# VectorE's port operations wait for GpSimd's turn, as GpSimd's already wait for VectorE's

## The chip, the cores and the metric

The kernel runs on one core of one Trainium2 chip. A core has five engines that run side by side, each through its own list of instructions in order: TensorE (PE in the profile, its weight loads apart as PEld), VectorE (DVE), ScalarE (ACT), GpSimd (POOL) and SyncE (SP, which only issues DMAs here). They wait for each other by semaphores. The metric is the device time of one execution in microseconds; the time before is the median of three runs.

## The reference

Attention over 8 batches of 8 heads (576 rows, head size 64), in which every score further than `tau` below its row's largest is left out, and behind it a gated mix: a causal convolution of 5 taps over the attention's output makes a gate, and two 512x512 products make the output.

```python
# attention: q, k, v are (8, 8, 576, 64)
scores = scale * q @ k.T
thresh = max(scores, axis=-1) - tau
scores = where(scores >= thresh, scores, -1e9) - max(scores)
attn = exp(scores) / (sum(exp(scores)) + 1e-9)
x = (attn @ v)            # heads joined: (8, 576, 512)
# mix
gate = sigmoid(sum(conv_w[k] * xp[:, k:k + 576] for k in range(5)))
out = (gate * (x @ w_val)) @ w_out
```

## The kernel before, in words

Two heads make a pair; a batch has four pairs. For a pair, TensorE makes tiles of 128 rows of scores (line 641) in PSUM, where four buffers called `u` serve everything that TensorE writes. VectorE scales each tile into `sb` and takes its largest value in the same instruction (`largest`, line 651). ScalarE makes the exponential `e` (670 and 672). What lies under the threshold is then left out in one of two ways: on VectorE (`keep`, line 689: reads `sb` and `e`, writes `pp` or `pl`) or on ScalarE (`bend`, 683). TensorE transposes the result (782), ScalarE or VectorE copies it to SBUF as `T` (794), TensorE multiplies it with `v` (855, or 826 in the first pairs), and VectorE brings the product to SBUF as `xT` (864 or 832).

The mix splits each float32 operand into a high and a low part, for products in three passes: `xh`, `xl` of `xT` (361 or 898, and 904 on GpSimd), `gh`, `gl` of the gated value (1074, and 1082 on GpSimd). The first tap of the convolution is on GpSimd (917), further ones on VectorE (`tap`, 922: reads `xT` and `pre`, writes `pre`); some of the first batches' are on GpSimd (937, 943). The products of a batch (line 1013) run on TensorE among the score tiles of the next batch. In the first 150 us the weights too are put together from 64-bit words, on VectorE (374 to 387), ScalarE and GpSimd (385, 390, 436). GpSimd also makes some thresholds `th` (663) and widens reciprocals (`inv`, 722).

The order of all this is made by a planner. Each operation is recorded with its engine, a cost and a due time, and `carry_out` plays them out on a model of the engines in which VectorE's operations on SBUF alone (engine name "DVEp": lines 374 to 387, 689 and 922) and all of GpSimd's ("POOL") take turns at one shared `port`. The instructions are then written out in that planned order. Beyond the waits that the data need, `carry_out` adds one kind of wait by hand: each operation on GpSimd also waits for the DVEp operation that the plan put last before it. VectorE's operations that read PSUM (651, 794, 864, 1051, 1115) have no part in the turns.

Of the kernel before, what the change touches and what calls it, by code (L numbers as in the profile page):

```python
# [35 lines left out]
for x in range(6):  # L36
# [10 lines left out]
    s=3,  # L47
# [19 lines left out]
    turn=-4538.24, copy=-712.99, attend=-3389.02, evac=-2135.73, fetch=1749.39, high_k=-1420.92,  # L67
# [13 lines left out]
def tile_thresholded_attention_gated_mix(  # L81
# [104 lines left out]
    port = [0.0]  # L186
# [16 lines left out]
    def keep_busy(room, n, x=ident):  # L203

        for _ in range(n):
            nc.tensor.matmul(room[:, 0:P], x, x, start=True, stop=True, skip_group_check=True)

    def sent(t, n, latency, each):

        at = t  # L210
        for _ in range(n):
            if len(landings) >= 8:
                at = max(at, landings[-8])
            wire[0] = max(wire[0], at + latency) + each
            landings.append(wire[0])
            at += SEND
        return at - t, wire[0] - t

    def carry_out():
        done_ops = []  # L220
        while True:
            best = None
            for e, ops in open_ops.items():
                can = []
                free = idle[e.rstrip("p")]
                if e in ("DVEp", "POOL"):
                    free = max(free, port[0])
                for o in ops:
                    if all(r.times for r in o.takes):
                        can.append((max([free, o.ready] + [r.times[0] for r in o.takes]), o))  # L230
                if can:
                    t = min(x for x, _ in can)
                    o = min((x[1] for x in can if x[0] <= t), key=(lambda o: o.due + AVOID * CHANGE.get((shape[0], o.shape), 0.0)) if e == "PE" else lambda o: o.due)
                    if best is None or (t, o.due) < (best[0], best[1].due):
                        best = (t, o, e)
            if best is None:
                break
            t, o, e = best
            for x in o.ways:
                open_ops[x].remove(o)  # L240
            if e == "PE" and 0.0 < idle["PE"] and t < FILL_UNTIL:
                pause = t - idle["PE"]
                if pause > 0.5:
                    o.fill = int((pause - 0.25) / 0.24)
            cost, done, emit = o.ways[e]
            if e == "PE" and cost:
                extra = CHANGE.get((shape[0], o.shape), 0.0)
                cost, done = cost + extra, done + extra
                shape[0] = o.shape
            if isinstance(done, tuple):  # L250
                cost, done = sent(t, *done)
            o.port = e if e in ("DVEp", "POOL") else None
            if o.port:
                port[0] = t + cost
            e = e.rstrip("p")
            idle[e] = t + cost
            o.landed, o.engine = t + done, e
            done_ops.append((o, emit))
            for r in o.takes:
                r.times.pop(0)  # L260
            for r, _ in o.gives:
                r.times.append(o.landed)
                r.times.sort()
            for n in o.next:
                n.ready = max(n.ready, idle["PE"] if e == "PE" and e in n.ways else o.landed)
                n.waits -= 1
                if not n.waits:
                    for x in n.ways:
                        open_ops[x].append(n)
        assert not any(open_ops.values()), "some operations can never begin"  # L270
        emitting.append(True)
        shared = None
        for o, emit in done_ops:
            if o.fill and r_right.live:
                keep_busy(r_right.live[-1][:, 1, PAST :], o.fill)
            n = len(nc.cur_bb.bb.instructions)
            emit()
            made = [x for x in nc.cur_bb.bb.instructions[n:]] if o.port else ()
            if made and o.port == "POOL" and shared:
                tc.add_manual_dep(  # L280
                    made[0], shared.name, mybir.DependencyInfo(mybir.DependencyClass.Sync, mybir.DependencyReason.DATA),
                    reason="VectorE's turn at the shared port is over",
                )
            elif made and o.port == "DVEp":
                shared = made[0]
            for rooms, room in o.gives:
                rooms.give(room(), o.landed)

# [245 lines left out]
    class Tile:  # L534
        s = None
# [65 lines left out]
        def room(self):  # L601

            if self.s is None:
                self.s = self.grp.second
            return self.s
# [555 lines left out]
    at = 0  # L1161
# [6 lines left out]
    for t in jobs:  # L1168
# [21 lines left out]
        if t.pair.g == NP - 1:  # L1190
            last = products(batch, len(tiles), last)
    carry_out()


# [57 lines left out]
```

## Time and profile before

| what | value |
|---|---|
| median of 3 runs | 684.32 us (684.11 to 684.62) |
| the profiled execution's own time | 684.27 us |
| its span, first to last instruction | 682.5 us |
| TensorE busy | 663.4 us, 97% of the span |
| VectorE busy | 604.1 us, 89% |
| ScalarE busy | 556.9 us, 82% |
| GpSimd busy | 223.1 us, 33% |
| TensorE's granted clock | 0.999 of full speed |

The 1.8 us between the profiled execution's time and its span lie outside the instructions. A busy engine is not always one that sets the time: a busy share is an average over stages. Which engine is waited for is read from the chain of waits and from the timeline.

### The profile page before, as it was taken

The numbers are of one execution on the slowest core, as the hardware profiler recorded it, in microseconds if no ns is written. First come the engines' busy times: TensorE is split into PE (matmuls) and PEld (weight loads), VectorE is DVE, ScalarE is ACT, GpSimd is POOL, SyncE is SP. The second block draws the span as 40 slices with busy tenths as digits, with TensorE's granted clock in tenths as the row PEclk, the third lists the DMA queues.
The fourth block names the chain that finished last, engine by engine and source line by source line (L and its number), as shares of the span: only waits on it lengthen the run. The fifth ranks groups of instructions, "written<-read, shape, count | busy, mean of one in ns | idle before, by whom it ended". The sixth has DMA issues, their size and how long they took to land.

```text
span 682.5 us, 21511 instructions
## 1 busy us (share of the span) xinstructions
PE 663.4 (97%) x8668; PEld 527.7 (77%) x8668; DVE 604.1 (89%) x1592; ACT 556.9 (82%) x1152; POOL 223.1 (33%) x383
## 2 busy tenths in 40 slices
PE   9999899989999999999999999999999999999997
PEld 6566566786887778888787788877788887877897
DVE  6999999977999999999999998998999999999742
ACT  6999999996878898787878888888987878788420
POOL 1454543565132421233222322324213332223131
PEclk9999999999999999999999999999999999999999
DMA  7133332321322223223321223221232233210002
GB/s 271 52 117 100 117 119 86 118 69 54 123 88 88 72 71 122 69 87 105 122 83 43 87 103 122 88 88 48 95 112 79 87 105 120 65 63 2 37 36 70
DMA packets 21075, 61.18 MB, mean 90 GB/s; under 512 B 2928, under 2 KB 4336, under 8 KB 20976
## 3 DMA queue, kind: packets, MB, share of 16 engines
q1 hardware_dynamic: 20832, 59.62, 25.8%
q8 instruction: 68, 1.11, 0.7%
q14 instruction: 31, 0.25, 0.1%
q10 hardware_dynamic: 144, 0.20, 0.1%
HBM read 50.37 MB, written 9.44 MB: 88 GB/s over the span
## 4 chain that ended last, share of the span: by engine, by line
PE 70%; DVE 15%; ACT 9%; issue 2%; DMA 0%; POOL 0%; DVEq 0%; ACTq 0%
PE u L1013 29%; PE u L641 18%; PE u L855 15%; PE u L782 8%; DVE sb L651 4%; DVE pre L922 3%; ACT T L794 3%; DVE pp L689 2%; ACT e L672 2%; ACT e L670 1%; ACT pp L683 1%; DVE T L794 1%; DVE g L1051 1%; DVE xT L864 1%; DVE sums L708 0%
## 5 line engine op out<-in xcount | busy, mean ns | idle before, releaser
L651 DVE TENSOR_SCALAR_CACHE_REDUCE sb<-u,sc 128x576 f32<-128x576 f32 x288 | 229.0, 810 | 14.8 <-PE u L641 10.7
L641 PE MATMUL u<-k,q 64*128 64x288 f32 x1240 | 192.9, 421 | 6.6 <-DVE sb L651 2.2
L670 ACT ACTIVATE e<-sb,th 128x576 f32<-128x576 f32 x165 | 124.7, 770 | 29.2 <-DVE th L663 21.0
L855 PE MATMUL u<-T,v 128*64 128x256 f32 (+1 forms) x1080 | 136.7, 408 | 0.7 <-DVE sb L651 0.7
L641 PEld LDWEIGHTS u<-k,q 64*128 64x128 f32 x1240 | 108.7, 188 | 27.3 <-DVE sb L651 7.3
L683 ACT ACTIVATE pp<-e,minus 128x576 f32<-128x576 f32 x142 | 109.6, 772 | 22.9 <-DVE pp L689 22.3
L782 PEld LDWEIGHTS u<-ident,pp 64*128 64x128 f32 x2304 | 99.0, 139 | 29.9 <-ACT pp L683 5.1
L855 PEld LDWEIGHTS u<-T,v 128*64 128x64 f32 x1080 | 75.2, 137 | 59.6 <-ACT T L794 6.5
L794 ACT COPY T<-u 128x768 f32<-128x768 f32 (+1 forms) x162 | 110.4, 699 | 11.0 <-PE u L782 9.8
L782 PE MATMUL u<-ident,pp 64*128 64x64 f32 x2304 | 109.4, 225 | 3.5 <-ACT T L794 0.9
L922 DVE SCALAR_TENSOR_TENSOR pre<-xT,cw,pre 128x576 f32<-128x576 f32 x121 | 100.5, 832 | 2.4 <-POOL pre L943 1.4
L689 DVE SCALAR_TENSOR_TENSOR pp<-sb,th,e 128x577 f32<-128x577 f32 x114 | 97.2, 856 | 3.8 <-ACT e L672 3.0
L672 ACT ACTIVATE e<-sb,nm 128x576 f32<-128x576 f32 x123 | 93.9, 771 | 0.2
L1013 PE MATMUL u<-gh,woh 64*128 64x288 f32 x512 | 88.9, 332 | 0.6 <-ACT seen L1001 0.3
L1013 PE MATMUL u<-xh,wvh 64*128 64x288 f32 x512 | 88.2, 326 | 0.5 <-ACT seen L1001 0.4
L794 DVE COPY T<-u 128x512 f32<-128x512 f32 (+1 forms) x94 | 73.9, 792 | 9.7 <-ACT e L670 5.0
L1082 POOL TENSOR_TENSOR gl<-g,gh 128x288 fp32r<-128x288 f32 x64 | 51.0, 803 | 89.8 <-DVE sums L708 34.4
L1013 PE MATMUL u<-xh,wvl 64*128 64x288 f32 x512 | 79.8, 292 | 0.0
L1013 PE MATMUL u<-xl,wvh 64*128 64x288 f32 x512 | 79.6, 292 | 0.0
L1013 PE MATMUL u<-gh,wol 64*128 64x288 f32 x512 | 78.8, 292 | 0.0
L1013 PE MATMUL u<-gl,woh 64*128 64x288 f32 x512 | 78.7, 292 | 0.0
L722 POOL TENSOR_SCALAR inv<-r 128x128 f32<-128x128 f32 x64 | 20.0, 312 | 159.8 <-DVE r L712 65.6
(95 smaller groups left out, 1037.8 us busy)
## 6 DMA issues: line engine op xcount, KB each, us to landing
q<-qT SPq DMA_DIRECT2D x31, 608.0 KB, 3.9
k<-kT SPq DMA_DIRECT2D x31, 496.0 KB, 4.8
v<-vs SPq DMA_DIRECT2D x32, 320.0 KB, 2.9
outT<-o SPq DMA_DIRECT2D x28, 288.0 KB, 2.1
pre<-w_val SPq DMA_DIRECT2D x4, 512.0 KB, 5.9
pre<-w_out SPq DMA_DIRECT2D x4, 512.0 KB, 3.3
outT<-o SPq DMA_DIRECT2D x8, 144.0 KB, 1.8
pp<-first SPq DMA_DIRECT2D x2, 192.0 KB, 3.0
```

The lines of the kernel that those rows point to most:

```text
L641: nc.tensor.matmul(row(self.s)[:, a, :], t.q[rows, x : x + P], t.k[rows, k0 : k0 + HS], start=i == 0, stop=h is not None or i == 1, skip_g ...
L651: nc.vector.tensor_scalar(self.sb[:, :S].rearrange("p (a f) -> p a f", a=2), row(self.room()), sc, None, op0=ALU.mult, op1=ALU.min, accum_ ...
L670: nc.scalar.activation(y, x, AF.Prelu, bias=self.grp.th[:, i : i + 1], scale=-1.0, alpha=STEEP)
L672: nc.scalar.activation(y, x, AF.Exp, bias=self.grp.nm[:, i : i + 1], scale=-1.0)
L683: nc.scalar.activation(grp.p[:, i * S : (i + 1) * S], self.e[:, :S], AF.Exp, bias=minus, accum_out=grp.sums[:, i : i + 1])
L689: nc.vector.scalar_tensor_tensor(grp.p[:, i * S : (i + 1) * S + 1], self.sb, grp.th[:, i : i + 1], self.e, op0=ALU.is_le, op1=ALU.mult, ac ...
L782: nc.tensor.transpose(tp[:, r, i * APART_BY : i * APART_BY + D], x[rows, :], ident[rows, rows])
L794: engine(T[:, c0 : c0 + n, self.off : self.off + P].rearrange("p c (r q) -> p r c q", r=2), tp)
L855: nc.tensor.matmul(a[hs, : W[half.j]], t.v[:, c0 : c0 + D], half.T[:, 2 * NKC if c == NKC else h * NKC + c, 0 : W[half.j]], start=c == 0, ...
L922: engine.scalar_tensor_tensor(cv, pair.xT[:, i + a : i + z], cw[:, g, i : i + 1], cv, op0=ALU.mult, op1=ALU.add)
L1013: nc.tensor.matmul(made["room"][:, to, 0:HS], wt[rows, c, e * P : (e + 1) * P], moving(c, i)[rows, parts[j]], start=turn == c == n == 0, s ...
L1082: engine.tensor_sub(gs[e][1][:, c], g[x][:, c], gs[e][0][:, c].bitcast(F32))
```

## The change

Before, only GpSimd's operations had the added wait. Now the same rule holds for both sides: `carry_out` remembers the last operation at the port, of whichever engine, and when the engine changes, the new one's first instruction waits for that operation. For GpSimd this is the wait that it had (a second operation in a row needs none, since it follows its own engine's first). New are the waits of VectorE's port operations for the GpSimd operation that the plan puts ahead of them. No instruction is added, removed or moved to another place on its engine.

```diff
             made = [x for x in nc.cur_bb.bb.instructions[n:]] if o.port else ()
-            if made and o.port == "POOL" and shared:
-                tc.add_manual_dep(
-                    made[0], shared.name, mybir.DependencyInfo(mybir.DependencyClass.Sync, mybir.DependencyReason.DATA),
-                    reason="VectorE's turn at the shared port is over",
-                )
-            elif made and o.port == "DVEp":
-                shared = made[0]
+            if made:
+                if shared and shared[0] != o.port:
+                    tc.add_manual_dep(
+                        made[0], shared[1].name,
+                        mybir.DependencyInfo(mybir.DependencyClass.Sync, mybir.DependencyReason.DATA),
+                        reason="the other engine's turn at the shared port is over",
+                    )
+                shared = (o.port, made[0])
```

In the built program, 99 rows of VectorE's list held a wait for GpSimd before, and 146 do now. In 140 places a VectorE instruction now has to see the end of a later GpSimd operation than it had to before; in some of these the row reads alike, because it waited for an earlier GpSimd operation already. All 140 are at lines 374 to 387, 689 and 922.

The first place is on VectorE in the fifth batch: the taps of one pair (`pre0<-xT0`, line 922) among the score tiles of the next. Before (in brackets, the engines that a row waits for; Activation is ScalarE, Pool is GpSimd):

```order
L922 SCALAR_TENSOR_TENSOR pre0_151<-xT0_138,cw0_176,pre0_151 128x576 [waits DVE_49]
L708 TENSOR_SCALAR sums2_124<-sums2_124 128x1 [waits Activation_49]
L651 TENSOR_SCALAR sb1_107,nm2_112<-u1_95,sc_78 128x576 [waits PE_49]
L712 RECIPROCAL r2_129<-sums2_124 128x2 [waits DVE_49]
L922 SCALAR_TENSOR_TENSOR pre0_151<-xT0_138,cw0_176,pre0_151 128x576
L689 SCALAR_TENSOR_TENSOR pp1_119,sums1_123<-sb0_106,th0_114,e1_105 128x577 [waits Activation_49]
```

Now (every line number below the change is one higher):

```order
L923 SCALAR_TENSOR_TENSOR pre0_151<-xT0_138,cw0_176,pre0_151 128x576 [waits DVE_49]
L709 TENSOR_SCALAR sums2_124<-sums2_124 128x1 [waits Activation_49]
L652 TENSOR_SCALAR sb1_107,nm2_112<-u1_95,sc_78 128x576 [waits PE_49]
L713 RECIPROCAL r2_129<-sums2_124 128x2 [waits DVE_49]
L923 SCALAR_TENSOR_TENSOR pre0_151<-xT0_138,cw0_176,pre0_151 128x576 [waits Pool_49]
L690 SCALAR_TENSOR_TENSOR pp1_119,sums1_123<-sb0_106,th0_114,e1_105 128x577 [waits Activation_49]
```

The second tap here, which waited for nothing, now waits for GpSimd (for `gl1<-g1,gh1`, line 1082); the rows stand where they stood.

The second place is a little earlier on VectorE, behind another pair's attention. Before:

```order
L922 SCALAR_TENSOR_TENSOR pre1_152<-xT1_139,cw0_176,pre1_152 128x576
L712 RECIPROCAL r2_129<-sums2_124 128x2 [waits DVE_49]
L689 SCALAR_TENSOR_TENSOR pp1_119,sums1_123<-sb3_109,th2_116,e0_104 128x577 [waits Activation_49,Pool_49]
L922 SCALAR_TENSOR_TENSOR pre1_152<-xT1_139,cw0_176,pre1_152 128x576 [waits DVE_49]
L708 TENSOR_SCALAR sums1_123<-sums1_123 128x1 [waits Activation_49]
L712 RECIPROCAL r0_127<-sums1_123 128x2 [waits DVE_49]
L922 SCALAR_TENSOR_TENSOR pre1_152<-xT1_139,cw0_176,pre1_152 128x576
```

Now:

```order
L923 SCALAR_TENSOR_TENSOR pre1_152<-xT1_139,cw0_176,pre1_152 128x576 [waits Pool_49]
L713 RECIPROCAL r2_129<-sums2_124 128x2 [waits DVE_49]
L690 SCALAR_TENSOR_TENSOR pp1_119,sums1_123<-sb3_109,th2_116,e0_104 128x577 [waits Activation_49]
L923 SCALAR_TENSOR_TENSOR pre1_152<-xT1_139,cw0_176,pre1_152 128x576 [waits DVE_49]
L709 TENSOR_SCALAR sums1_123<-sums1_123 128x1 [waits Activation_49]
L713 RECIPROCAL r0_127<-sums1_123 128x2 [waits DVE_49]
L923 SCALAR_TENSOR_TENSOR pre1_152<-xT1_139,cw0_176,pre1_152 128x576 [waits Pool_49]
```

Two taps have got a wait for GpSimd (for `xl`, line 904, and for `gl`, line 1082), and the `keep` between them has lost its own, because the first tap now waits for the same engine later than it did.

## Rows read from the trace of the kernel before

**Rows 1.** Head of the page: span of the profiled execution.

```profile
span 682.5 us, 21511 instructions
```

**Rows 2.** Windows: from:to, length, then busy us of PE, PEld, DVE, ACT, POOL.

```profile
20.00:40.00 20.00, 19.67 (x222) 13.11 (x221) 18.85 (x55) 19.94 (x41) 10.19 (x16) 1.00 0.32 101
367.40:447.40 80.00, 79.45 (x1076) 64.62 (x1074) 74.35 (x194) 66.86 (x141) 23.07 (x43) 1.00 0.27 90
```

**Rows 3.** Line 922: count, shortest/median/longest ns, first and last start.

```profile
L922 DVE SCALAR_TENSOR_TENSOR pre<-xT,cw,pre x121: 793/814/1299, 33.8 to 655.0; 128x576 f32<-128x576 f32 x121
```

**Rows 4.** Timeline near 170 us: start, length, engine, line, [idle before <-releaser].

```profile
168.85 1.43 POOL L943 TENSOR_TENSOR pre<-pre,tmp 128x576 f32<-128x576 f32 x1
...
170.26 0.76 POOL L917 TENSOR_SCALAR pre<-xT,cw 128x576 f32<-128x576 f32 x1
...
170.31 1.30 DVE L922 SCALAR_TENSOR_TENSOR pre<-xT,cw,pre 128x576 f32<-128x576 f32 x1 [0.26 <-POOL pre L943]
```

**Rows 5.** Timeline: first and last of the 61 late places, VectorE's instruction.

```profile
11.44 0.18 DVE L380 TENSOR_SCALAR cw<-cw 128x20 int32<-128x20 int32 x1
...
653.35 0.81 DVE L922 SCALAR_TENSOR_TENSOR pre<-xT,cw,pre 128x576 f32<-128x576 f32 x1
```

**Rows 6.** Chain that ended last, 442 to 453 us: start, length, what.

```profile
442.52 0.75 DVE g L1051
...
450.42 0.60 DVE T L794
```

**Rows 7.** Timeline of the same place: GpSimd, VectorE, TensorE.

```profile
447.10 0.80 POOL L1082 TENSOR_TENSOR gl<-g,gh 128x288 fp32r<-128x288 f32 x1 [4.89 <-DVE sums L708]
...
447.75 0.80 DVE L922 SCALAR_TENSOR_TENSOR pre<-xT,cw,pre 128x576 f32<-128x576 f32 x1
...
451.07 0.76 PE L641 MATMUL u<-k,q 64*128 64x288 f32 x4 [0.22 <-DVE sums L708]
```

**Rows 8.** Timeline, 386 to 392 us: GpSimd, VectorE, TensorE.

```profile
386.04 0.73 POOL L904 TENSOR_TENSOR xl<-xT,xh 128x256 fp32r<-128x256 f32 x1
...
386.43 0.95 DVE L922 SCALAR_TENSOR_TENSOR pre<-xT,cw,pre 128x576 f32<-128x576 f32 x1
...
388.10 0.81 DVE L922 SCALAR_TENSOR_TENSOR pre<-xT,cw,pre 128x576 f32<-128x576 f32 x1
...
389.06 0.79 POOL L1082 TENSOR_TENSOR gl<-g,gh 128x288 fp32r<-128x288 f32 x1 [2.29 <-DVE pre L922]
...
389.50 0.97 DVE L922 SCALAR_TENSOR_TENSOR pre<-xT,cw,pre 128x576 f32<-128x576 f32 x1
...
390.79 0.94 DVE L794 COPY T<-u 128x768 f32<-128x768 f32 x1
...
392.03 0.51 PE L1013 MATMUL u<-gh,woh 64*128 64x288 f32 x2
392.37 0.30 PE L1013 MATMUL u<-gl,woh 64*128 64x288 f32 x2
```

**Rows 9.** Timeline, 151 to 159 us: GpSimd, VectorE, TensorE.

```profile
151.83 0.86 POOL L904 TENSOR_TENSOR xl<-xT,xh 128x320 fp32r<-128x320 f32 x1
...
152.05 3.44 DVE L922 SCALAR_TENSOR_TENSOR pre<-xT,cw,pre 128x576 f32<-128x576 f32 x4
...
155.58 1.42 POOL L943 TENSOR_TENSOR pre<-pre,tmp 128x576 f32<-128x576 f32 x1 [2.88 <-DVE sums L708]
156.96 0.25 POOL L361 TENSOR_SCALAR pl<-pl 128x64 f32<-128x64 f32 x1
...
157.03 0.82 DVE L922 SCALAR_TENSOR_TENSOR pre<-xT,cw,pre 128x576 f32<-128x576 f32 x1 [0.53 <-POOL pre L943]
...
158.64 1.57 PE L855 MATMUL u<-T,v 128*64 128x320 f32 x10 [0.73 <-DVE sb L651]
```

**Rows 10.** Timeline: first and last of five GpSimd operations behind a running VectorE one.

```profile
15.40 0.76 POOL L663 TENSOR_SCALAR th<-nm,less 128x1 f32<-128x1 f32 x1 [1.82 <-DVE r L712]
...
166.78 1.43 POOL L904 TENSOR_TENSOR xl<-xT,xh 128x320 fp32r<-128x320 f32 x1 [1.00 <-DVE pre L922]
```

## The prediction

> **What bounds the kernel now.** I read the windows first. In a period of 80 us, one of the batches in the middle that repeat, TensorE is busy 79.45 us and VectorE 74.35 us [rows 2]. So the middle is TensorE's, with 0.55 us to spare, and VectorE has 5.65 us. In the first 140 us it is otherwise: ScalarE is busy 19.94 of 20 us, TensorE 19.67 and VectorE 18.85 [rows 2]; there ScalarE sets the pace. Next I read the chain of waits, since a bound by busy time still passes through other engines. Once in each period it leaves TensorE: for 8.5 us, from 442.52 to 451.02, it runs over VectorE alone, without a gap, and gives back to TensorE behind a copy [rows 6]. What makes VectorE late there makes the end late. Last I read the timeline, for where a VectorE operation begins before the GpSimd operation has ended that it will now wait for.
>
> **What the change removes and adds.** It moves nothing. It adds 140 waits of VectorE, of which I paired each with the two instructions in the timeline. In 79 places GpSimd's operation had ended over 0.03 us before VectorE's began: these cost nothing as long as the two stay that far apart. In 61 it had not; the first and the last are in [rows 5], and 30 of them lie in the first 200 us.
>
> **The price of a late place.** A wait for GpSimd is short: VectorE starts at 170.31, 0.03 us behind GpSimd's end at 168.85 + 1.43 = 170.28 [rows 4]. A tap usually takes 0.814 us [rows 3]. So with the wait VectorE's end is 0.03 + 0.81 = 0.84 us behind GpSimd's. What is it without? The same instruction at 170.31 runs into GpSimd's next one, 170.26 to 171.02, takes 1.30 us and ends at 171.61, 0.59 us behind it [rows 4]. The two are kept apart already, but the blocked VectorE operation has its beginning behind it when the port comes free: the wait costs 0.84 - 0.59 = 0.25 us that the port doesn't. Where the overlap is under about 0.2 us nothing was lengthened, and the wait costs the overlap and 0.03 us more. For each of the 61 I took the later of its own start and GpSimd's end + 0.03, added its usual length, and subtracted its old end: 13.2 us in all, 7.5 of them in the first 200 us and 5.8 behind. That is VectorE's lateness if nothing takes it up, the upper bound of this term; the lower one is 0.
>
> [...]
>
> **What of it is on the path.** Behind a waiting instruction stands all of VectorE's list: the next tiles' `largest` (line 651), which frees a `u` for TensorE, the copies to `T` (794) and to `xT` (864).
>
> (a) In each period the tap at 447.75 lies in the stretch where the chain is VectorE's. GpSimd's `gl` ends at 447.10 + 0.80 = 447.90; the tap may start at 447.93 and ends at 448.74, not at 448.55 [rows 7]. Nothing takes the 0.19 us up: the next three instructions and the copy follow each other without a gap, and the copy ends at 451.02 [rows 6], and TensorE, idle for 0.22 us, starts 0.05 us behind that, at 451.07 [rows 7]. Six such places, 208 to 608 us: 1.1 us.
>
> (b) In each period there is a pair of late taps, at 386.43 and 389.50. The first may start at 386.04 + 0.73 + 0.03 = 386.80 and ends at 387.61, not at 387.38; the tap at 388.10 follows 0.23 us late and ends at 389.14. GpSimd's `gl` waits for that one already: it begins 0.15 us behind its end [rows 8], now at 389.29, and ends at 390.08. So the tap at 389.50 starts at 390.11 and ends at 390.92, not at 390.47: 0.45 us late, for the wait goes to and fro. The copy at 390.79 ends at 392.18, not at 391.73. TensorE's products start at 392.03 [rows 8], 0.30 us behind the old end; in (a) 0.05 were enough. So they may be 0.20 us late. But their first row takes 0.51 us and the next one 0.30 [rows 8], so the first may have stood 0.21 us in the queue for the array anyway. Between 0 and 0.20 us I take 0.10, the row deciding for neither; six places: 0 to 1.2, taken as 0.6 us.
>
> (c) At 152.05 four taps begin under GpSimd's `xl`, which ends at 152.69: by the price above, about 0.23 us more here, all four end that much later. GpSimd's addition at 155.58 follows the taps and ends at 157.00 + 0.23; GpSimd's `pl`, 0.25 us long, follows that one, and the tap at 157.03, which waited only for the addition, now waits for `pl` too: until about 157.47. That is 0.44 us; the `largest` behind it frees what TensorE has been waiting for 0.73 us, at 158.64 [rows 9]. 0.4 us, once.
>
> (d) The other 28 places of the first 200 us hold about 6.9 us. VectorE has 1.15 us idle in 20 us there, and ScalarE has none [rows 2], so most of it lies beside ScalarE's work; bounds 0 and 6.9. I take 0.6, near the lower end for that reason.
>
> (e) The other places of a period, some 0.3 us, lie in VectorE's 5.65 us of idle time [rows 2]. If that cover went, each would cost up to 0.25 us.
>
> Sum: 1.1 + 0.6 + 0.4 + 0.6 = 2.7 us. The profiled execution took 684.27 us, with a span of 682.5 us [rows 1], and lies 0.05 us under the median, 684.32. Forecast: **687.0 us**, 0.4% slower; with (a) and (c) alone 685.8, with (b) at 1.2 and (d) at 4 of its 6.9 us, 691.
>
> **The rivals.** This kernel's runs tell a change from none at about 0.2%, 1.4 us.
>
> *Lateness is taken up (no change), 684.3 to 685.7.* For it: VectorE is not the bound by busy time, and 0.55 us of TensorE's idle time in a period [rows 2] hide 0.19 us if TensorE isn't short of buffers. Against: (a) and (c) sit where TensorE is seen waiting. [...] Chance of both 0.17.
>
> *Waits go to and fro: over 691.* Since GpSimd waits for VectorE and VectorE for GpSimd, a late operation on either makes the other late, as in (b) and (c), and places that are early now become late. With all 13.2 us on the path 697.5 us. Against: in the middle VectorE's idle time, 5.65 us a period, is over five times the lateness there (5.8 us in some six periods). Chance 0.08.
>
> *Faster.* In five places of the first 170 us GpSimd began while VectorE held the port, out of the plan's turn, and was held up itself: a threshold at 15.40 took 0.76 us, an `xl` at 166.78 took 1.43 us [rows 10] where the same shape takes 0.86 [rows 9]; these are the first and the last of the five. Against the usual lengths of their kinds they lose 2.5 us together; now GpSimd goes first. If these thresholds and reciprocals are what ScalarE and TensorE wait for in the stretch that ScalarE bounds, and none of (a) to (d) comes through: 681.8 us. It decides from 1.4 us net. Against: (a) alone takes back 1.1. Chance 0.07.
>
> That the change does nothing is excluded: the waits stand in the built program.
>
> **The numbers.** Forecast 0.68 (685.7 to 691), taken up 0.17, to and fro 0.08, faster 0.07. So slower by over 0.2% 0.76, within 0.2% 0.17, faster 0.07. The range leaves out the two outer cases and the lowest part of the second: 684.6 to 691 us.
>
> **What would show it.** Right: no tap or `keep` is longer than 0.85 us; in the stretch of (a) VectorE idles for GpSimd once a period, about 0.2 us; in (c) TensorE's 0.73 us become about 1.15; a period takes 80.2 to 80.4 us; GpSimd's five operations have their usual lengths. Wrong: the period stays at 80.0 while VectorE's idle time for GpSimd grows, which says that (a) is taken up; or the loss lies in the first 140 us, which says that (d) was put too low.

## The result, and the profile after

The changed kernel takes 689.36 us (median of 4 runs, 689.29 to 689.45), beside 684.47 us (684.11 to 684.88) for the kernel before on the same chip: a ratio of 1.0074 [1.0062, 1.0086]. It is slower by 4.9 us, 0.7%. The forecast was 687.0 us in a range of 684.6 to 691.0, so the direction and the range held, and the forecast itself lay 2.4 us low.

The head of the page after, to compare with [rows 1]:

```profile
span 687.5 us, 21491 instructions
```

Two windows after, beside [rows 2]; the second one is the same period, 4.3 us later at its start and 4.5 at its end (from:to, length, then busy us of PE, PEld, DVE, ACT, POOL):

```profile
20.00:40.00 20.00, 19.47 (x220) 12.85 (x217) 18.26 (x56) 19.60 (x40) 10.18 (x16) 1.00 0.30 101
371.70:451.90 80.20, 79.43 (x1076) 64.31 (x1074) 73.88 (x194) 66.97 (x142) 23.08 (x43) 1.00 0.26 90
```

In the first window all three busy engines have lost time: TensorE 0.20 us, VectorE 0.59, ScalarE 0.34. ScalarE, which had 0.06 us idle in 20, now has 0.40. In the period VectorE is busy 0.47 us less, because the time for which a tap or a `keep` was held up under GpSimd's operation counted as busy and a wait doesn't (in the period the lines of the tap and the `keep` are busy 13.30 and 11.19 us before, 13.03 and 10.68 after): a lower busy share is no gain here.

The taps after, beside [rows 3] (shortest, median and longest ns), and one of the reasons for which VectorE sat idle before them (us, times; these six are the second taps of (b)):

```profile
L923 DVE SCALAR_TENSOR_TENSOR pre<-xT,cw,pre x121: 806/816/822, 34.3 to 660.2; 128x576 f32<-128x576 f32 x121
...
  POOL gl L1083: 2.1, 6
```

The longest tap takes 0.822 us, not 1.299. No tap is blocked any more, and the time stands as idle time in front of it.

The place (a) on the timeline after, beside [rows 7]: GpSimd, VectorE, TensorE (start, length, engine, line, [idle before <-releaser]):

```profile
451.34 0.80 POOL L1083 TENSOR_TENSOR gl<-g,gh 128x288 fp32r<-128x288 f32 x1 [4.88 <-DVE sums L709]
...
452.18 0.82 DVE L923 SCALAR_TENSOR_TENSOR pre<-xT,cw,pre 128x576 f32<-128x576 f32 x1
...
455.52 0.76 PE L642 MATMUL u<-k,q 64*128 64x288 f32 x4 [0.44 <-DVE sums L709]
```

GpSimd ends at 452.14 and the tap starts at 452.18. From GpSimd's start to the tap's it was 0.65 us, now 0.84: 0.19 us, as worked out. TensorE's idle time grows from 0.22 to 0.44 us. This is the place as predicted.

The pair of (b) after, beside [rows 8]:

```profile
390.24 0.73 POOL L905 TENSOR_TENSOR xl<-xT,xh 128x256 fp32r<-128x256 f32 x1
391.01 0.82 DVE L923 SCALAR_TENSOR_TENSOR pre<-xT,cw,pre 128x576 f32<-128x576 f32 x1
...
393.50 0.79 POOL L1083 TENSOR_TENSOR gl<-g,gh 128x288 fp32r<-128x288 f32 x1 [2.53 <-DVE pre L923]
...
394.33 0.82 DVE L923 SCALAR_TENSOR_TENSOR pre<-xT,cw,pre 128x576 f32<-128x576 f32 x1 [0.36 <-POOL gl L1083]
...
396.47 0.40 PE L1014 MATMUL u<-gh,woh 64*128 64x288 f32 x2
396.71 0.30 PE L1014 MATMUL u<-gl,woh 64*128 64x288 f32 x2
```

The wait does go to and fro: tap, GpSimd's `gl`, tap, each behind the other. But TensorE's first row of products takes 0.40 us where it took 0.51, and the second one starts at 396.71, 4.34 us later than before, when the score tile ahead of it was already 4.29 us late: the pair costs 0.05 us.

The place (c) after, beside [rows 9]:

```profile
154.88 0.87 POOL L905 TENSOR_TENSOR xl<-xT,xh 128x320 fp32r<-128x320 f32 x1
155.78 3.00 DVE L923 SCALAR_TENSOR_TENSOR pre<-xT,cw,pre 128x576 f32<-128x576 f32 x4 [0.60 <-POOL xl L905]
...
160.25 0.24 POOL L362 TENSOR_SCALAR pl<-pl 128x64 f32<-128x64 f32 x1
160.53 0.82 DVE L923 SCALAR_TENSOR_TENSOR pre<-xT,cw,pre 128x576 f32<-128x576 f32 x1 [0.74 <-POOL pl L362]
...
162.14 2.91 PE L856 MATMUL u<-T,v 128*64 128x320 f32 x20 [1.09 <-DVE sb L652]
```

The tap starts behind GpSimd's `pl`, and TensorE idles 1.09 us instead of 0.73.

And GpSimd's two operations of [rows 10]:

```profile
15.37 0.27 POOL L664 TENSOR_SCALAR th<-nm,less 128x1 f32<-128x1 f32 x1 [1.99 <-DVE r L713]
...
170.25 0.87 POOL L905 TENSOR_TENSOR xl<-xT,xh 128x320 fp32r<-128x320 f32 x1 [1.00 <-DVE pre L923]
```

They take 0.27 and 0.87 us instead of 0.76 and 1.43: GpSimd now goes first, as worked out.

**Where the 4.9 us are.** I follow four rows of TensorE through every profile: A, score products at the start (line 625, `u<-pp,pl`, 8.12 us before, in the profile of the kernel before), B, a transposition that waits for VectorE's reciprocal (line 782, 151.48), C and D, the ends of (c) and of (a) in [rows 9] and [rows 7] (158.64 and 451.07). In the kernel before it takes 143.36 us from A to B, 7.16 from B to C and 292.43 from C to D. A and B before, and after:

```profile
8.12 1.19 PE L625 MATMUL u<-pp,pl 64*64 64x288 f32 x8
...
151.48 0.53 PE L782 MATMUL u<-ident,pp 64*128 64x64 f32 x10 [0.33 <-DVE r L712]
```

```profile
7.61 1.19 PE L626 MATMUL u<-pp,pl 64*64 64x288 f32 x8
...
154.53 0.53 PE L783 MATMUL u<-ident,pp 64*128 64x64 f32 x10 [0.45 <-DVE r L713]
```

After, A starts at 7.61, so A to B takes 146.92 us: 3.56 more. B to C takes 0.45 more and C to D 0.95 more. The table says the same of every kernel below; times are medians, beside 684.4 to 684.5 us for the kernel before. The ratio goes by all runs of both kernels and so need not be the quotient of the medians.

| kernel | time, us | ratio to before | A | A to B | B to C | C to D |
|---|---|---|---|---|---|---|
| after | 689.36 | 1.0074 [1.0062, 1.0086] | 7.61 | +3.56 | +0.45 | +0.95 |
| early | 688.18 | 1.0051 [1.0034, 1.0067] | 8.27 | +3.41 | +0.46 | +0.22 |
| late | 685.99 | 1.0023 [1.0012, 1.0035] | 7.92 | +0.03 | +0.01 | +0.91 |
| passed | 685.37 | 1.0009 [1.0000, 1.0019] | 7.42 | +1.29 | +0.02 | +0.48 |
| not_passed | 688.65 | 1.0057 [1.0040, 1.0073] | 8.12 | +2.40 | +0.46 | +0.96 |
| slow_vector | 684.81 | 1.0006 [0.9997, 1.0015] | 8.40 | +0.44 | 0.00 | +0.05 |
| slow_vector2 | 687.25 | 1.0051 [1.0039, 1.0064] | 8.55 | +2.66 | +0.01 | -0.05 |
| slow_scalar | 690.32 | 1.0086 [1.0072, 1.0099] | 8.51 | +5.19 | -0.01 | +0.29 |
| nowaits | 690.52 | 1.0090 [1.0076, 1.0104] | 7.76 | -0.79 | +0.63 | +3.64 |
| one_way | 686.75 | 1.0040 [1.0027, 1.0053] | 7.71 | +0.58 | +0.84 | +1.08 |
| late_turns | 683.44 | 0.9990 [0.9981, 0.9999] | 7.77 | -0.83 | +0.01 | +0.08 |
| cut_once | 689.43 | 1.0070 [1.0056, 1.0084] | 8.62 | +2.90 | +0.44 | +0.91 |

A itself moves by up to 1.2 us from one profile to the next, whatever the kernel (last section), so single times are compared behind A. How well two profiles agree from there on is seen in late, whose program up to 190 us is that of before: from A to B it stays within 0.06 us of it, at points 20 us apart.

### The profile page after: what moved, and what is told of

Its sections match the earlier page's. It is cut to its first block, busy times and chain, and to the rows that moved or that the text cites. A ratio compares the mean times of both kernels' runs of the same rounds, so it can differ in the third digit from the quotient of the medians.

```text
span 687.5 us, 21491 instructions
## 1 busy us (share of the span) xinstructions
PE 663.3 (96%) x8668; PEld 526.3 (77%) x8668; DVE 599.8 (87%) x1592; ACT 558.6 (81%) x1152; POOL 220.6 (32%) x383
## 4 chain that ended last, share of the span: by engine, by line
PE 71%; DVE 13%; ACT 7%; POOL 3%; issue 2%; DMA 0%; DVEq 0%; POOLq 0%
PE u L1014 29%; PE u L642 18%; PE u L856 15%; PE u L783 8%; DVE pre L923 4%; DVE sb L652 3%; DVE pp L690 3%; ACT T L795 2%; ACT e L671 2%; ACT pp L684 1%; ACT e L673 1%; PE u L827 1%; DVE T L795 1%; POOL gl L1083 1%; DVE xT L865 1%
## 5 line engine op out<-in xcount | busy, mean ns | idle before, releaser
L923 DVE SCALAR_TENSOR_TENSOR pre<-xT,cw,pre 128x576 f32<-128x576 f32 x121 | 98.4, 815 | 9.3 <-POOL pre L918 2.2
L690 DVE SCALAR_TENSOR_TENSOR pp<-sb,th,e 128x577 f32<-128x577 f32 x114 | 92.7, 816 | 11.3 <-POOL xl L905 4.7
```

Source lines behind the costliest of these rows:

```text
L690: nc.vector.scalar_tensor_tensor(grp.p[:, i * S : (i + 1) * S + 1], self.sb, grp.th[:, i : i + 1], self.e, op0=ALU.is_le, op1=ALU.mult, ac ...
L923: engine.scalar_tensor_tensor(cv, pair.xT[:, i + a : i + z], cw[:, g, i : i + 1], cv, op0=ALU.mult, op1=ALU.add)
```

## The experiments

Theory 1 was that VectorE's lateness by itself comes through to TensorE in the first 150 us, which makes the prediction's term (d) too small. Against it stood theory 2, that there the changed order costs, where GpSimd now goes first, and later theory 3, that GpSimd carries the lateness on, because each engine waits for the other.

**One stretch alone.** All of these change one condition of the changed kernel: which instructions get the added wait. `o.landed` is the time at which the plan has the operation's result.

```diff
-if shared and shared[0] != o.port:
+if shared and shared[0] != o.port and (o.port == "POOL" or o.landed < 190):    # early
+if shared and shared[0] != o.port and (o.port == "POOL" or o.landed > 190):    # late
```

Expected of early: 

> The added waits of VectorE stand only where the plan puts the instruction before 190 us (30 of the 61 late places); behind that the program is that of before. Theory 1: VectorE's lateness in the first 140 us comes through to TensorE, because VectorE follows itself there without a gap, and the (d) of the prediction was mis-sized: 3.4 us by 150 us and 0.6 us at place (c), so about 688.3 us (687.8 to 688.8) against 684.5 before. Rival: the sizes of the prediction for (c) and (d) hold (0.4 + 0.6 us), and the middle costs the rest: 685.5 us.

Expected of late: 

> The added waits stand only where the plan puts the instruction behind 190 us (31 late places). Theory 1: places (a) at 0.21 us and (b) at 0.05 us, six each, less 0.08 us that each period gives back: 685.5 us (685.2 to 685.9); a period takes 80.15 to 80.2 us. Rival (the middle carries what the first 140 us don't): 688 us or more. With early the two gains over before should add up to the 4.9 us of the change, if the places act one by one.

Measured: +3.7 and +1.5 us on their own kernel before; 5.2 together, against 4.9 for both. The places add up; late, at 685.99 us, lies just above its expected 685.2 to 685.9. Early loses 3.41 us between A and B, where the prediction had allowed 0.6 for its term (d), and late loses nothing there. So the term (d) is what was mis-sized. In late, the four places (a) and the three pairs (b) that lie between C and D cost 0.91 us; the prediction's sizes give 4 x 0.19 + 3 x 0.10 = 1.06.

**The changed order.** In six places of the first 170 us GpSimd's operation had gone second and now goes first. In five, the prediction's, VectorE's operation had held it up (in one of these, at 95.53, GpSimd's row starts 0.10 us ahead of VectorE's and still takes 0.81 us where it takes 0.27 after); in the sixth, at 11.51, it had begun 0.07 us behind VectorE's start and had its usual 0.27 us.

```diff
+first = round(o.landed, 2) in (10.05, 14.53, 56.41, 93.47, 118.3, 165.58)
+if shared and shared[0] != o.port and (o.port == "POOL" or first):        # passed
+if shared and shared[0] != o.port and (o.port == "POOL" or not first):    # not_passed
```

Expected of passed: 

> Only six of the added waits are left: those where GpSimd had begun behind VectorE's operation before and now goes first (planned at 10.05, 14.53, 56.41, 93.47, 118.3 and 165.58 us). Theory 2: the changed order is what costs in the first 140 us: 687 to 688 us. Theory 1 (every late place counts by its lateness; these six hold 3.5 of the 7.5 us of the first 200 us, and give GpSimd's operations back 2.5 us): 685.3 us (684.6 to 686.2). The prediction's rival 'faster' : under 683.5 us.

Expected of not_passed: 

> All added waits but those six. Theory 1: 688.5 us (687.8 to 689.2), since the other places carry most of the lateness and (c), (a) and (b) are all left. Theory 2 (the changed order costs 2.5 to 3.5 us): 686 to 686.8 us.

Measured: +0.9 and +4.2 us. The six places alone cost 1.29 us between A and B and the others 2.40, together 3.69 where the change has 3.56. Theory 2 falls: the changed order isn't the main cost, since about two thirds of the loss come without it. So does the prediction's rival "faster": GpSimd has its operations back at their usual lengths and the time is not lower.

**The price by itself.** A kernel of its own, with VectorE's tap behind GpSimd's subtraction of `gl`'s shape, begun under it, and then with the wait:

Expected: 

> A kernel of its own that leaves out the whole computation: 128 steps, in each of which a GpSimd operation on SBUF begins and, behind 0 to 12 small writes, a VectorE operation on SBUF; every kind once without and once with the wait, all twice. Theory 1: without a wait a tap of VectorE that begins well under GpSimd's operation ends 0.59 to 0.62 us behind GpSimd's end, with it 0.84 us, so the wait costs 0.22 to 0.25 us; begun less than 0.2 us ahead of GpSimd's end it costs the overlap and 0.03 us. Rival (the blocked instruction runs its whole length when the port comes free): 0.81 and 0.84 us, a price of 0.03 us.

Timeline of two of its steps, the first without a wait and the second with it; line 48 is GpSimd's, line 52 VectorE's:

```profile
15.31 0.79 POOL L48 TENSOR_TENSOR gl<-g,gh 128x288 fp32r<-128x288 f32 x1 [0.72 <-DVE fill L67]
15.50 1.22 DVE L52 SCALAR_TENSOR_TENSOR pre<-xT,cw,pre 128x576 f32<-128x576 f32 x1
16.82 0.79 POOL L48 TENSOR_TENSOR gl<-g,gh 128x288 fp32r<-128x288 f32 x1 [0.71 <-DVE tick L61]
17.65 0.82 DVE L52 SCALAR_TENSOR_TENSOR pre<-xT,cw,pre 128x576 f32<-128x576 f32 x1 [0.92 <-POOL gl L48]
```

By these rows the tap ends without the wait at 16.72, 0.62 us behind GpSimd's end at 16.10, and with it at 18.47, 0.86 us behind 17.61. Over all steps in which the tap began behind GpSimd's operation (0.01 to 0.19 us behind its start) the two are 0.60 to 0.61 and 0.85 to 0.86 us, whatever the overlap and with either of two GpSimd operations: the wait costs 0.24 to 0.25 us. For VectorE's multiplication of one input (128x576, 0.46 us) they are 0.31 and 0.50: 0.18 us. The price of 0.25 us stands. Overlaps of under 0.2 us were not reached here, since the small writes follow each other too closely (twelve of them take 0.40 us); that half of the price was not tried.

So the tap is held up under GpSimd's operation, as the prediction has it. By the rival all of it would be left at GpSimd's end, and the change would have cost nearly nothing. It ends 0.61 us behind, not 0.82.

**Lateness without a wait.** Is it that VectorE is late, or that it waits for GpSimd? The kernel before, with extra work in front of the 35 VectorE instructions planned between 26 and 146 us that the change makes wait (the lines that make the scratch tiles are left out):

```diff
+if o.port == "DVEp" and shared and shared[0] == "POOL" and 26 < o.landed < 146:
+    for x in slow: nc.vector.memset(x, 0.0)     # slow_vector: four tiles of 128x1
+    for x in slow: nc.scalar.copy(x, less)      # slow_scalar, instead: two tiles of 128x1
+    nc.vector.memset(slow, 0.0)                 # slow_vector2, instead: one tile of 128x288
```

Expected of slow_vector: 

> The kernel before, without any added wait of VectorE, but with four small writes of VectorE to a scratch column (59 ns each by the trace of before, together 0.24 us) ahead of the 35 VectorE instructions planned between 26 and 146 us that the change makes wait: 8.3 us of lateness on VectorE and nothing to do with GpSimd. Theory 1 (in this stretch VectorE's lateness comes through to TensorE): 4 to 7 us, 688.5 to 691.5 us. The prediction's step (it lies beside ScalarE's work): at most 1.5 us, 684.5 to 686 us.

Expected of slow_scalar: 

> The same 35 places, but the lateness put on ScalarE: two small copies there (0.14 to 0.2 us each by the trace of before, together 0.3 to 0.4 us, 10 to 14 us in all). The prediction's step (ScalarE sets the pace before 140 us): nearly all of it comes through, 693 to 698 us. Theory 1 in its strict form (VectorE sets the pace, and ScalarE follows it): at most 4 us, 684.5 to 688.5 us. Between the two: the engines pass the work round in a ring, and lateness on either comes through in part.

Expected of slow_vector2: 

> The first attempt put only about 0.06 us on VectorE a place, since its small writes ran into each other. Here one write of 128x288 to a scratch tile stands ahead of each of the 35 VectorE instructions, about 0.25 us by the rows of 128x576 (0.54 us) and 128x128 (0.17 us): some 8.5 us of lateness on VectorE between 26 and 146 us, and no wait for GpSimd. Theory 1 (VectorE's lateness comes through there by itself): 4 to 7 us, 688.5 to 691.5 us. Theory 3 (VectorE alone has gaps in front of ScalarE's results that take it up; the change costs more because GpSimd carries the lateness over these gaps): at most 2.5 us, 684.5 to 687 us.

slow_vector cost nothing that can be measured, but it put hardly any lateness on VectorE. Timeline of one place, the three further writes beside the tap that follows:

```profile
51.47 0.06 DVE L278 MEMSET slow<- 128x1 f32 x1
51.48 0.81 DVE L927 SCALAR_TENSOR_TENSOR pre<-xT,cw,pre 128x576 f32<-128x576 f32 x1
51.48 0.08 DVE L278 MEMSET slow<- 128x1 f32 x3
```

Four writes of 59 ns each start some 0.01 us apart and run beside the tap; my 0.24 us had added lengths that overlap. It tells nothing of the theories. In slow_vector2 one longer write stands there:

```profile
40.19 0.30 DVE L277 MEMSET slow<- 128x288 f32 x1
40.42 0.69 DVE L926 SCALAR_TENSOR_TENSOR pre<-xT,cw,pre 128x576 f32<-128x576 f32 x1
```

The write takes 0.30 us, the tap starts 0.23 us behind its start and is then 0.69 us long, where the usual tap has 0.81. To know what that adds I took, at each of the 35 places, the time from the end of VectorE's instruction ahead to the end of the tap or `keep`, and subtracted the same time in the kernel before: 0.19 us where nothing else is in play, and 4.12 us in all, not 8.5, since at some of the written places VectorE had been held up by GpSimd's operation before and now loses less (the `keep` at 32.70 us took 1.21 us, and takes 1.02 at 33.77). The time, 2.9 us more, lies between what theory 1 (688.5 us and more) and theory 3 (687 and less) were given, but for half the lateness that they were given it for. TensorE loses 2.66 us of these 4.12 between A and B, 65%. For the changed kernel the same sum over the places before B is 5.7 us (6.1 added and 0.4 taken away), and it loses 3.56, 62%; not_passed has 3.82 and loses 2.40, 63%. (passed doesn't fit in: 2.3 added, 1.6 taken away, and 1.29 lost.) So VectorE's lateness comes through to about six tenths, with a new wait for GpSimd or without one. The share depends on what is taken away: of the additions alone, 5.7 us in slow_vector2 and 6.1 in the changed kernel, it is 47% and 58%. And in all of these kernels GpSimd still waits for VectorE.

In slow_scalar two copies of ScalarE stand there:

```profile
28.63 0.27 ACT L278 COPY slow<-less 128x1 f32<-128x1 f32 x2
28.80 1.44 ACT L677 ACTIVATE e<-sb,nm 128x576 f32<-128x576 f32 x2
```

By the same subtraction they add 0.18 us a place and 6.24 us in all, not the 10 to 14 expected, and TensorE loses 5.19 of it, 83%. The time, 690.32 us, lies between the two expected ranges. ScalarE's share is the larger, so the prediction's reading of the stretch has something in it, but VectorE isn't covered by it.

**To and fro.** Theory 3 was that GpSimd, which waits for VectorE, carries VectorE's lateness over gaps in which VectorE would have lost it.

```diff
+if shared and shared[0] != o.port and (o.landed < 190 if o.port == "DVEp" else o.landed > 190):    # one_way
+if shared and shared[0] != o.port and (o.port == "DVEp" or not 38 < o.landed < 50):                # cut_once
```

Expected of one_way: 

> As early (VectorE's added waits only in what is planned before 190 us), but GpSimd's added waits are taken away in the same stretch, so that VectorE waits for GpSimd and GpSimd no longer for VectorE; behind 190 us the program is that of before. Theory 3 (the lateness goes to and fro): most of the 3.7 us that early cost is gone, 684 to 686 us. Theory 1 (each late VectorE operation costs by itself): 687 us or more.

Expected of cut_once: 

> The changed kernel, but GpSimd's added waits are left out for what is planned between 38 and 50 us (four instructions: lines 362, 386, 723 and 918 of the changed kernel). In the changed kernel TensorE loses 0.65 us between 45 and 50 us, at a keep of VectorE (line 690) that waits for GpSimd's line 391, and 0.12 us more by 52 us. Theory 3 (VectorE's lateness of 0.7 us reached that keep only because GpSimd had waited for VectorE, line 386, and carried it over VectorE's idle 1.06 us): the 0.65 us of that place are gone, TensorE's loss between 45 and 52 us is at most 0.3 us, and GpSimd's line 391 ends at least 0.5 us ahead of the keep's other wait. Theory 1 (VectorE's own lateness comes through): the 0.65 us stay. The whole differs too little for the time to tell: 688.4 to 689.4 us.

The place of cut_once in the kernel before (GpSimd, TensorE, GpSimd, VectorE, TensorE):

```profile
44.25 1.28 POOL L385 TENSOR_TENSOR wvh<-wvh,o 128x512 fp32r<-128x512 f32 x1 [1.99 <-DVE pp L689]
...
45.04 2.38 PE L826 MATMUL u<-T,v 128*64 128x256 f32 x20
...
45.75 1.28 POOL L390 TENSOR_TENSOR whole<-whole,wvh 128x512 f32<-128x512 f32 x1
...
46.89 0.82 DVE L689 SCALAR_TENSOR_TENSOR pp<-sb,th,e 128x577 f32<-128x577 f32 x1 [1.06 <-ACT e L672]
...
48.25 0.26 PE L782 MATMUL u<-ident,inv 64*128 64x64 f32 x2
```

And after:

```profile
44.97 1.27 POOL L386 TENSOR_TENSOR wvh<-wvh,o 128x512 fp32r<-128x512 f32 x1 [2.09 <-ACT T L795]
...
45.62 2.38 PE L827 MATMUL u<-T,v 128*64 128x256 f32 x20 [0.27 <-DVE sb L652]
...
46.47 1.28 POOL L391 TENSOR_TENSOR whole<-whole,wvh 128x512 f32<-128x512 f32 x1
...
47.78 0.82 DVE L690 SCALAR_TENSOR_TENSOR pp<-sb,th,e 128x577 f32<-128x577 f32 x1 [1.23 <-POOL whole L391]
...
49.13 0.28 PE L783 MATMUL u<-ident,inv 64*128 64x64 f32 x2
```

Here VectorE is 0.72 us late, and its lateness reaches TensorE in two ways. At once: TensorE waits for VectorE's `largest` at 45.62, 0.58 us later than before, where it had stood 0.24 us late. And through GpSimd: line 386 waits for VectorE (its row names ScalarE's `T`, which ends about when VectorE's `keep` does; before, GpSimd began here ahead of the end of that `T`, so that isn't what it needs), 391 follows it 0.72 us late, and the `keep` at 47.78, which before had 1.06 us to spare for ScalarE's `e`, waits for 391. In cut_once GpSimd has no added wait there:

```profile
44.92 1.71 POOL L386 TENSOR_TENSOR wvh<-wvh,o 128x512 fp32r<-128x512 f32 x1 [1.35 <-ACT pre L948]
...
46.86 1.27 POOL L391 TENSOR_TENSOR whole<-whole,wvh 128x512 f32<-128x512 f32 x1
...
48.16 0.83 DVE L690 SCALAR_TENSOR_TENSOR pp<-sb,th,e 128x577 f32<-128x577 f32 x1 [0.93 <-POOL whole L391]
```

GpSimd begins under VectorE's operation, is blocked itself (1.71 us instead of 1.27), and line 391 ends 0.03 us ahead of the `keep` again, not 0.5 us ahead of its other wait: that part of the expectation missed. From the transposition ahead of 45 us on to 52 us TensorE loses 0.31 us instead of 0.77, and between A and B 2.90 instead of 3.56. So one place of this kind is worth some 0.5 us. one_way, without GpSimd's waits in the whole stretch, loses 0.58 us between A and B where early loses 3.41; but behind B it loses 0.84 and 1.08 us (at (c) GpSimd's line 944, without its turn, begins under VectorE's taps and takes 1.93 us), and the time, 686.75 us, lies between the 686 at most of theory 3 and the 687 at least of theory 1. And part of the gain between A and B isn't VectorE's at all: without any added wait that stretch is 0.79 us shorter than before.

So one_way has to be set beside late_turns (below), which has GpSimd's waits taken away there too and no added wait of VectorE. Against it one_way loses 0.58 + 0.83 = 1.41 us up to B, where early, against the kernel before, loses 3.41. It is clearest up to the row of TensorE that stands at 80 us in the kernel before, where late_turns is only 0.02 us off that kernel: counted from A, early is 2.00 us late there and one_way 0.27. So more than half of early's loss needs GpSimd's waits beside VectorE's, as theory 3 has it, and some 1.4 us of it VectorE's waits cost alone. slow_vector2 doesn't speak against that, since GpSimd waits for VectorE in it as in the kernel before. Two things aren't separated here: without GpSimd's waits the late places put less on VectorE (3.2 us up to B instead of 5.6, by the same subtraction, over all of VectorE's operations at the port), and less of it comes through (44% instead of 61%).

**No turns at all.** GpSimd's added waits removed too, everywhere (nowaits) or in what is planned before 146 us (late_turns), with no added wait of VectorE:

```diff
+if False:                                                                                  # nowaits
+if shared and shared[0] != o.port and (o.port == "POOL" and o.landed > 146):               # late_turns
```

Expected of nowaits: 

> All waits that the plan adds by hand are gone, GpSimd's too. Theory 1 (a wait costs about 0.25 us of the waiting engine's time where the port would have blocked it anyway): on GpSimd, which has time, the waits cost nothing, and without them GpSimd begins under VectorE's operations and holds up some of them: 684.5 to 687 us. Rival (the turns themselves cost, on either engine): 682 to 683.5 us.

Expected of late_turns: 

> The kernel before with GpSimd's added waits only in what is planned behind 146 us, and no added wait of VectorE. In the run without any added waits TensorE stood 0.8 us earlier by 150 us (the landing of the first transfers taken off) and lost 6.5 us from there on: so about 683.6 us, 0.8 us faster than before. Rival (the 0.8 us are given back at the places behind 150 us, where the chain passes through another engine): 684.4 us.

Without turns the middle is far worse, 3.64 us between C and D, and the time, 690.52 us, lies above both expected ranges (682 to 683.5 and 684.5 to 687). Timeline of nowaits, GpSimd and VectorE at the place (a):

```profile
368.51 1.56 POOL L1083 TENSOR_TENSOR gl<-g,gh 128x288 fp32r<-128x288 f32 x2 [4.67 <-ACT gh L1075]
...
369.44 1.25 DVE L923 SCALAR_TENSOR_TENSOR pre<-xT,cw,pre 128x576 f32<-128x576 f32 x1
```

GpSimd runs both `gl` at once, and the tap, begun under the second one, takes 0.4 us longer (1.25 us instead of 0.81), on the stretch where VectorE's chain sets the end. That such places make up the 3.64 us is read from the rows and not tried by itself. GpSimd's waits are worth 7 us behind B (690.52 against 683.44 us for late_turns, which has them there). Ahead of B they cost 0.8: without them GpSimd's results come earlier. late_turns keeps the one part and drops the other: 683.44 us, a ratio of 0.9990 [0.9981, 0.9999]. That is 0.9 us less than before, as its trace says between A and B (-0.83), and it beats both kernels, by little. In its expectation, "the landing of the first transfers" should be read as the first products of TensorE (last section).

## Why the prediction was right, and where it was too small

- **The price**, 0.25 us a late place, held to 0.01 us (price). The sum of lateness from it held as well, about 5.7 us before B.
- **(a)**, six places at 0.19 us on the path: right in mechanism and size, 0.19 us on VectorE and 0.21 us on TensorE in a period. TensorE's 0.44 us of idle time there are the old 0.22 and the new.
- **(b)**, between 0 and 0.20 us, taken as 0.10: it is 0.05. The bound was right, and the rows agree with its reason, the first row of products standing in the queue (it takes 0.40 us instead of 0.51).
- **(c)**, 0.44 us: measured 0.45.
- **(e)**, nothing: right. Four places (a) at 0.21 and three pairs (b) at 0.05 us are 0.99 us; C to D shows 0.95. From one tap of (a) to the same one a period later it is 79.9 us before and 80.1 after, 0.19 more.
- **(d)** is the term that was mis-sized: taken as 0.6 us of 6.9, it measured 3.56 us up to B, and some 0.1 us between C and 200 us. The step that failed is "VectorE has 1.15 us idle in 20 us there, and ScalarE has none, so most of it lies beside ScalarE's work". The 1.15 us are those of one window, 20 to 40 us, and don't hold for the stretch. Another window of it, and the whole, in the kernel before (columns as in [rows 2]):

```profile
80.00:100.00 20.00, 18.50 (x220) 12.22 (x218) 19.73 (x56) 19.59 (x39) 8.80 (x14) 1.00 0.32 100
20.00:140.00 120.00, 113.01 (x1332) 78.35 (x1330) 113.58 (x324) 118.58 (x231) 54.74 (x85) 1.00 0.31 101
```

From 80 to 100 us VectorE is idle for 0.27 us, less than ScalarE's 0.41; over the whole stretch VectorE has 5% idle and TensorE 6%. Nor do busy shares carry the conclusion: lateness on ScalarE comes through to 83% and on VectorE to 62 to 65%. TensorE, VectorE and ScalarE wait for each other in turn (a `u` to write, its `largest`, the exponential, the `keep`), and through its added waits GpSimd is on that ring as well: with them taken away in that stretch, VectorE's waits cost 1.41 us and not 3.41 (one_way). That the ring passes the lateness on in this way is read from single places, not shown for the whole. The prediction had named the sign for this step, a loss in the first 140 us. A term between 0 and 6.9 us that no row decides should have been put in the middle; with 3.6 for 0.6 the forecast is 690.0 us. The range held because its upper end gave (d) 4 us, not because the forecast had its size.
- What was measured adds up: (a) 1.3, (b) 0.3, (c) 0.45 and (d) 3.7 us are 5.7, where the span is 5.0 us longer and A starts 0.51 us earlier than in the profile before, 5.5 together. What is over lies in the middle, where a period is 0.19 us longer and not 0.26.
- **The rivals.** "Taken up", and a price of only 0.03 us a place, which shares its chance of 0.17, fall by the price run, 0.24 to 0.25 us. "To and fro" doesn't take the time over 691, but its mechanism is at work: at single places (46.9, and (b)), and up to B in more than half of what early loses. "Faster" falls by passed: no gain with these places alone (1.0009 [1.0000, 1.0019]).

ScalarE was the busiest engine in that stretch (118.58 of 120 us), and its lateness did cost the most, 83%. That the others are then covered was the prediction's step, and for VectorE the runs show that it isn't.

## What to carry to other kernels

Here VectorE's tap, begun 0.01 to 0.19 us behind the start of GpSimd's operation, is held up without any wait and ends 0.61 us behind that operation's end; a semaphore in front of it makes that 0.86 us, so it costs the start that the held instruction has behind it by then, 0.25 us a place (0.18 us for a multiplication of one input). Whether that pays depended on the side and on the stretch: on GpSimd's side, behind 150 us, where VectorE's chain is on the path once a period, it saves 7 us; ahead of 150 us it cost 0.8 there; on VectorE's side it cost 4.9. Whether lateness on an engine is covered could not be read here, where engines wait for each other in turn, from busy shares, least of all from those of one window; a few writes of known length in front of the instructions in question measure it (and their worth on the engine is the difference from end to end, not the length in the trace: 0.19 us a place here, for writes of 0.30).

## What the runs showed of the hardware

A GpSimd operation that begins under VectorE's tap is held up in the same way, and also has its start behind it: in the price kernel it ends 0.65 us behind the tap's end where the free one takes 0.79, and 0.53 where it takes 0.67. Two rows of it:

```profile
4.55 0.82 DVE L52 SCALAR_TENSOR_TENSOR pre<-xT,cw,pre 128x576 f32<-128x576 f32 x1
4.62 1.39 POOL L48 TENSOR_TENSOR gl<-g,gh 128x288 fp32r<-128x288 f32 x1 [4.18 <-DVE tick L61]
```

Row A differs by 1.2 us between profiles, 7.42 to 8.62, and the difference stays to the end. It is not the transfers, whose first use (line 519) begins at 3.46 to 3.56 us in the four profiles below, but TensorE: its first eight score products take 2.12 us in the profile before, 1.35 in passed, 2.29 in cut_once and 1.53 after, behind the same twelve products of 2.93 us:

```profile
4.03 2.12 PE L625 MATMUL u<-pp 64*128 64x288 f32 x8
```

```profile
4.10 1.35 PE L626 MATMUL u<-pp 64*128 64x288 f32 x8
```

```profile
4.01 2.29 PE L626 MATMUL u<-pp 64*128 64x288 f32 x8
```

```profile
4.11 1.53 PE L626 MATMUL u<-pp 64*128 64x288 f32 x8
```

The longer the eight take, the later is A: 7.42 (passed), 7.61 (after), 8.12 (before) and 8.62 us (cut_once). By the trace's starts a pair of these products follows the other every 0.48 us at first and every 0.24 us later, half the pace and then the whole. After, the change lies within the eight (pairs at 4.11, 4.72, 4.98 and 5.22 us); in the kernel before all eight go at half the pace (4.03, 4.64, 5.12 and 5.61). The trace's record of TensorE's granted clock begins, at 1.00, at 4.74 us after and at 5.86 before, about where the pace changes, and the only other level on record is 0.50, at the very end of both (from 687.40 and 681.70 us on). That the clock stood at 0.50 in the slow part is the author's estimate from the pace: no clock is on record there. (A window's clock reads 1.00 there too, as from 0 to 4 us.) Why the pace changes at another time in each profile stays open; nothing was tried on it. The difference is of the size of the scatter between times of one kernel on one chip (683.35 to 684.82 us for 15 runs of the one before); on two others single runs of it reached 686.0 and 687.9 us.
